# One DMA group moved ahead of another on SyncE, and a higher cap on the products that fill TensorE's idle times

## The chip, the cores and the metric

The kernel runs on one core of a Trainium2 chip. The metric is the device time of one execution in microseconds; lower is better. Five executions of the kernel before gave 496.59, 498.37, 501.29, 503.88 and 504.88, so the median is 501.29.

## The reference

Two blocks follow one another. The first is a delta rule over 4 batches, 8 heads, 768 time steps, with heads 48 wide; the second sends each of the 3072 resulting rows of 384 to one of 8 experts, picked by a hash of its token id.

```python
for t in range(S):
    y[:, :, t] = einsum('bhd,bhde->bhe', q[:, :, t], state)
    v_old = einsum('bhde,bhd->bhe', state, k_n[:, :, t])
    state = state + beta[:, :, t] * einsum('bhd,bhe->bhde', k_n[:, :, t], v[:, :, t] - v_old)
x = y.transpose(0, 2, 1, 3).reshape(3072, 384)
expert = token_ids * 2654435761 % 8
for e in range(8):
    out[expert == e] = maximum(x[expert == e] @ w1[e], 0) @ w2[e]
```

The weights are 8 x 384 x 1024 and 8 x 1024 x 384, all in float32.

## The kernel before, in words

**The delta rule (the first 224 us).** The 768 steps are cut into 24 chunks of 32 steps, and four chunks make a group. The four batches lie side by side on the 128 partitions. Ahead of the chunks of a group come:

- the loads of its keys and queries (`load_turn`, L427 to L431), on SyncE's queue,
- their turning by TensorE against a unit matrix (`turn`, L449 to L463), which ScalarE copies to the tiles KQ,
- the gram products, key by key and query by key (`gram`, L468 to L512; for group 0 `first_gram`, L514 to L539), copied to the tiles GK and GQ, and masked by VectorE,
- the inverse of a triangular matrix per chunk and head, 31 steps of two instructions on VectorE (`inverse`, L572 to L632), and a turning back to the tile TU (L638).

A chunk then is a chain (`chunk`, L672 to L803). TensorE asks the state with the keys (L659) on top of the values (L690), and ScalarE copies the result to R (L695). TensorE multiplies with the inverse (L709), and ScalarE copies W (L723). TensorE updates the state (L738), and ScalarE copies the new state to S (L762). Beside this chain stand the spreading of TU and GQ to Tz and MT (L550), the asking with queries (L659), the answer (L779) and its copy (L788). GpSimd scatters the rows to a scratch tensor in DRAM, ordered by expert (L794). The last four chunks are split in halves, with VectorE's help (L699, L764).

**The planner.** All this isn't issued as written. Each step is noted as a task with an engine, an estimated duration and its dependences (`task`, L253). The function `order` (L286 to L424) plays a list schedule over the estimates, and the tasks are then emitted in the order of their planned starts (L1188 to L1200). The planner also estimates when TensorE's next block of 256 instructions has been loaded. It counts the instructions issued so far in `issued`, and a task whose instructions lie in a block that isn't there yet starts later (L381 to L390).

Where the planner expects TensorE to be idle before a task, `fill` (L320 to L337) puts in products of the unit matrix with itself that nobody reads, 128 to 512 columns wide, as long as an unused PSUM bank is there; they are emitted at L1192.

**The first expert** (`first_expert`, L982 to L1080) runs at the end of this stage, mostly after the last chunk. It takes the first 18 chunks' rows early, and the other rows late. The hidden values of the late part, `h_late`, lie in the same SBUF tile, `xqs[0]` (L144), that later holds the rows of every second expert; the last reader of `h_late` is the product at L1075.

**The other experts (256 to 484 us).** For each expert, `gemm1` (L1222) makes eight blocks of hidden values, each from three products. The max with zero is ScalarE's for even blocks (L1229) and VectorE's for odd ones (L1231). Behind every odd block VectorE also turns a third of the next expert's rows (`turn`, L1290; `turn_x`, L107). Four banks are used in turn, so block 7 needs the bank that VectorE emptied of block 3.

`fetch` (L1283) reads the row at which an expert's rows begin into a register of SyncE, and issues four DMAs for the rows (L100) and one for their numbers (L104). `load_w` (L111) reads which expert it is, and issues four DMAs for w1 (L94) and one for w2 (L117), 384 KB each and 1536 KB. All of these go out on SyncE's queue in program order. Ahead of the loop this order is (L1303 to L1308): rows of the second expert, its weights, weights of the third expert, rows of the third expert, and a register with the number of extra rounds.

The rows of the second expert go to `xqs[1]`; those of the third go to `xqs[0]`.

Of the kernel before, what the change touches and what calls it, by code (L numbers as in the profile page):

```python
# [20 lines left out]
def kernel(  # L21
# [27 lines left out]
    RANKS = [4, 0, 1, 2, 3, 5, 6, 7]  # L49
# [35 lines left out]
    def value(at, engine, top):  # L85
        return nc.values_load(ov_i[0:1, at:at + 1], engines=[engine], min_val=0, max_val=top)

    def expert_at(rank, engine):
        return value(AT_E + rank, engine, E - 1)

    def w1_parts(e, w1_sb, eng):

        w1 = moe_w1[bass.ds(e, 1)].rearrange("o d f -> (o d) f")
        return [lambda j=j: eng.dma_start(  # L94
            out=w1_sb[C * j:C * j + C],
            in_=w1[QD * j:QD * j + QD].rearrange("(c d) f -> d c f", d=C)) for j in range(4)]

    def load_x(row, blocks, xq, eng):
        rows = x_dram[bass.ds(row, C * blocks)].rearrange("(i t) x -> t i x", t=C)
        return [eng.dma_start(out=xq[C * j:C * j + C, 0:blocks, 0:QD],  # L100
                              in_=rows[:, :, QW * j:QW * j + QD]) for j in range(4)]

    def load_numbers(row, cols, width, to, eng):
        return eng.dma_start(out=to, in_=x_dram[bass.ds(row, cols * width), QD:QD + 1].rearrange(  # L104
            "(c p) x -> p c x", c=cols))
# [5 lines left out]
    def load_w(e, pool, eng):  # L111
        s2 = moe_w2[bass.ds(e, 1)].rearrange("o f d -> (o f) d")
        w1_sb = pool.tile([P, CO, F], F32, name="w1_sb")
        for part in w1_parts(e, w1_sb, eng):
            part()
        w2_sb = pool.tile([P, FO, DIN], F32, name="w2_sb")
        eng.dma_start(out=w2_sb, in_=s2.rearrange("(fo p) d -> p fo d", p=P))  # L117
        return w1_sb, w2_sb
# [40 lines left out]
    with ExitStack() as phase1:  # L159
# [126 lines left out]
        def order():  # L286
# [33 lines left out]
            def fill(i, idle, at):  # L320

                nonlocal issued
                rate = 1.67
                if at < 2000:

                    rate, idle = 3.34, idle - 900
                idle = min(idle, 2750 if at < 2000 else 1100)
                while idle > FILL_OVER and at < FILL_UNTIL:
                    unused = [b for b in range(len(homes)) if banks[b] is not None
                              and banks[b] <= at]  # L330
                    if not unused:
                        break
                    n = min(4, max(1, int((idle - 160) / (rate * P))))
                    fills.setdefault(i, []).append((unused[0], n))
                    issued += 2
                    idle -= n * rate * P
                    at += n * rate * P  # L337
# [17 lines left out]
            while len(done) < n:  # L355
                best, can = None, {}
                for e, r in ready.items():
                    can[e] = [(x, i) for x, i in ((when(x, i), i) for x, i in r)
                              if x is not None]
                    if can[e]:  # L360
                        at = max(free[e], min(x for x, _ in can[e]))
                        if best is None or at < best[0]:
                            best = (at, e)
                at, e = best
# [27 lines left out]
                if e == "PE":  # L392
                    fill(pick, s - free[e], free[e])
# [55 lines left out]
        def turn(g, a, b):  # L449
            KQ, src, job = KQs[g % 4], (KTs, QTs)[a][b], new_job(1, early=g < 3)  # L450

            def view():
                return bank(job).rearrange("p (u x) -> p u x", u=HU)

            def go():
                for u in range(HU):
                    nc.tensor.transpose(view()[:, u, :],
                                        src[:, u].rearrange("p r d -> p (r d)"), ident)

            task("PE", 540, (f"t{a}{b}",), (f"j{job}",), go, words=8, job=(job, 0))  # L460
            task("ACT", 490, (f"j{job}",), (f"KQ{g % 4}{a}{b}",),
                 lambda: nc.scalar.activation(KQ[:, :, a, b, :], view(), ACT.Copy),
                 job=(job, 0))  # L463
# [739 lines left out]
    with tc.tile_pool(name="w_pool2", bufs=2) as w_pool2, \  # L1203
# [18 lines left out]
        def gemm1(w1_sb, xT, h_sb, width, between=None):  # L1222
            for fo in range(FO):
                h_ps = hidden()
                for co in range(CO):
                    nc.tensor.matmul(h_ps[:, :width], lhsT=w1_sb[:, co, fo * P:(fo + 1) * P],  # L1226
                                     rhs=xT[:, co, :width], start=(co == 0), stop=(co == CO - 1))
                if fo % 2 == 0:
                    nc.scalar.activation(h_sb[:, fo, :width], h_ps[:, :width], ACT.Relu)  # L1229
                else:  # L1230
                    nc.vector.tensor_scalar(out=h_sb[:, fo, :width], in0=h_ps[:, :width],  # L1231
                                            scalar1=0.0, scalar2=None, op0=ALU.max)
                if between is not None:
                    between(fo)
# [16 lines left out]
        def send_rows(rows, idx, alone):  # L1251
            scat = nc.gpsimd.indirect_dma_start(  # L1252
                out=out[:, :], out_offset=bass.IndirectOffsetOnAxis(ap=idx, axis=0),
                in_=rows, in_offset=None, bounds_check=N - 1, oob_is_err=False)
            if alone:
                tc.declare_no_dep(scat.ins, group="scatters", reason="disjoint rows")
                tc.add_to_no_dep_group("scatters", scat.ins)
# [10 lines left out]
        def send(oT, e, col):  # L1268

            o_ps = results()  # L1270
            cw = CWS[e]
            for i in range(CO):
                nc.tensor.transpose(o_ps[0:cw, i * P:(i + 1) * P],
                                    oT[:, i, col * cw:(col + 1) * cw], ident)
            store(o_ps, col, cw, idx[e][0:cw, col:col + 1], True)
# [4 lines left out]
        def own(e):  # L1280
            return KTS[e], CWS[e], (CAPS[e] + C - 1) // C, xqs[RANKS.index(e) % 2]

        def fetch(e):  # L1283
            cols, cw, blocks, xq = own(e)
            row = value(AT_ROW + e, mybir.EngineType.SP, N)
            load_x(row, blocks, xq, nc.sync)
            xns[e] = m_i.tile([P, KT], F32, name="numbers")
            load_numbers(row, cols, cw, xns[e][0:cw, 0:cols, None], nc.sync)
# [13 lines left out]
        with tc.manual_schedule():  # L1302
            fetch(RANKS[1])  # L1303
            for part in parts:
                part()
            w_tiles[2] = load_w(expert_at(RANKS[2], mybir.EngineType.SP), w_pool2, nc.sync)
            fetch(RANKS[2])
            n_ov = nc.values_load(ov_i[0:1, NOV:NOV + 1], min_val=0, max_val=NOV)  # L1308
            for c in range(CO):
                turn(RANKS[1], c)  # L1310
            for k in range(SC):
                send_rows(o_first[:, k], idx_i[:, k:k + 1], True)
            send_rows(o_late, idx_i[:, SC:SC + 1], True)
            for i, e in enumerate(RANKS):
                if e == FIRST:
                    continue
                w1_sb, w2_sb = w_tiles.pop(i)
                rest = [e for e in RANKS[i + 1:i + 3]]
                done = RANKS[i - 1] if RANKS[i - 1] in oTs else None

                def between(fo):

                    to = max(3, i + 1)
                    if fo == 0 and to < E and to not in w_tiles:
                        w_tiles[to] = load_w(expert_at(RANKS[to], mybir.EngineType.SP),
                                             w_pool if to == 4 else w_pool2, nc.sync)
                    elif fo == 1 and len(rest) > 1:
                        fetch(rest[1])
                    if fo % 2 and fo // 2 < CO and rest:
                        turn(rest[0], fo // 2)  # L1330
                    if fo % 2 and done is not None:
                        send(oTs[done], done, fo // 2)

                h_sb = m_h.tile([P, FO, CAP], F32, name="h_sb")
                gemm1(w1_sb, xTs.pop(e), h_sb, CAPS[e], between)
                if KTS[e] > CO:
                    oTs[e] = m_t.tile([P, CO, CAP], F32, name="oT")
                    for j in range(CO):
                        gemm2_turned(w2_sb, h_sb, oTs[e], j, CAPS[e])
                else:  # L1340
                    cols, cw, _, _ = own(e)
                    for j in range(cols):
                        gemm2(w2_sb, h_sb, j, cw, idx[e][0:cw, j:j + 1], True)
# [49 lines left out]
```

## Time and profile before

| What | us |
|---|---|
| median of five executions | 501.29 |
| the profiled execution, its own time | 498.19 |
| its span, first to last instruction | 496.6 |
| TensorE busy | 460.4 |
| VectorE busy | 230.0 |
| ScalarE busy | 191.6 |
| GpSimd busy | 72.6 |
| mean granted clock of TensorE, as a share of full | 0.969 |

How to read it: busy times are unions of the instructions' spans on an engine. The engines work side by side, so they don't add up to the span. "PE" is TensorE's products and "PEld" its weight loads, "DVE" is VectorE, "ACT" ScalarE, "POOL" GpSimd and "SP" SyncE, whose instructions only issue DMAs. A float32 product stands in the trace as two records (a fill 512 wide is "x2"). An arrow in square brackets names what ended the idle time ahead of an instruction; "issue" means that nothing in the profile did.

### The profile page before, as it was taken

The page shows a single profiled execution, that of the slowest core. Times are in us where ns is not written, and L with a number is a line of the kernel's source. Part 1 is how long each engine was busy: PE and PEld are TensorE (multiplying, and loading weights), DVE is VectorE, ACT ScalarE, POOL GpSimd, SP SyncE. Part 2 cuts the span into 40 slices and gives each one's busy share as a digit, 9 for nine tenths or more (in the row PEclk, how much of TensorE's full clock was granted, in tenths as well). Part 3 has the DMA queues.
Part 4 walks back from the last instruction along what each step waited for, and adds up shares of the span by engine and source line. Part 5 has one row for each costly group of instructions (what it writes and reads, how often), then busy time and mean ns, then how long its engine had stood idle before and what let it go on. Part 6 is the DMA issues. An engine that isn't in the chain of part 4 may idle for free. (4 is left out here: it accounts for less than half of the span.)

```text
span 496.6 us, 15828 instructions
## 1 busy us (share of the span) xinstructions
PE 460.4 (93%) x6648; PEld 312.9 (63%) x6648; DVE 230.0 (46%) x720; ACT 191.6 (39%) x443; POOL 72.6 (15%) x106
## 2 busy tenths in 40 slices
PE   8982898999899999899999999999999999999990
PEld 5761686787677777787765555555555565655650
DVE  5899979998898889860102013012021130110100
ACT  4763778889699687541121011011010110100100
POOL 6000102122020022320020012113011022001010
PEclk9995799999999799999999999999999999999997
DMA  9996767568544457523999995745643016401010
GB/s 143 169 157 114 118 124 143 111 142 159 118 101 93 93 133 174 133 81 81 191 272 244 250 213 154 152 130 111 114 151 74 0 41 164 143 7 39 0 31 15
DMA packets 137181, 60.61 MB, mean 122 GB/s; under 512 B 123006, under 2 KB 131826, under 8 KB 137109
## 3 DMA queue, kind: packets, MB, share of 16 engines
q1 hardware_dynamic: 131572, 49.80, 49.9%
q0 software_dynamic: 5344, 9.66, 6.1%
q8 instruction: 53, 0.87, 0.7%
q10 hardware_dynamic: 192, 0.12, 0.2%
q14 instruction: 20, 0.16, 0.1%
HBM read 49.19 MB, written 10.42 MB: 120 GB/s over the span
## 5 line engine op out<-in xcount | busy, mean ns | idle before, releaser
L1263 PE MATMUL bank<-h_sb,w_sb 128*128 128x424 f32 (+1 forms) x192 | 66.4, 506 | 0.0
L624 DVE TENSOR_TENSOR tmp<-U,Ni 128x87 f32<-128x87 f32 (+15 forms) x186 | 62.5, 341 | 3.5 <-ACT U L608 0.2
L622 DVE TENSOR_TENSOR U<-U,tmp 128x87 f32<-128x87 f32 (+15 forms) x186 | 61.9, 338 | 2.9
L1252 POOL DMA_INDIRECT out_dram<-o_sb,tokens x25 | 29.3, 1171 | 197.8 <-ACT o_sb L1248 152.7
L1226 PE MATMUL z<-xT,w_sb 128*128 128x424 f32 (+3 forms) x168 | 57.4, 491 | 0.0
L1263 PEld LDWEIGHTS bank<-h_sb,w_sb 128*128 128x128 f32 x192 | 36.2, 190 | 28.4 <-issue 15.6
L794 POOL DMA_INDIRECT x_scratch<-x_sb,slot x24 | 24.9, 1039 | 182.7 <-ACT MT L550 58.4
L1231 DVE TENSOR_SCALAR h_sb<-z 128x424 f32<-128x424 f32 (+3 forms) x14 | 7.9, 562 | 88.7 <-PE z L1226 88.7
L1242 PE MATMUL bank<-w_sb,h_sb 128*121 128x384 f32 (+1 forms) x144 | 46.9, 486 | 0.0
L762 ACT ACTIVATE S<-psS 48x384 f32<-48x384 f32 (+1 forms) x92 | 42.7, 464 | 10.1 <-PE psS L738 8.8
L1226 PEld LDWEIGHTS z<-xT,w_sb 128*128 128x128 f32 x168 | 31.6, 190 | 22.2 <-issue 7.5
L1242 PEld LDWEIGHTS bank<-w_sb,h_sb 128*121 128x121 f32 (+1 forms) x144 | 26.6, 185 | 19.4
L779 PEld LDWEIGHTS psY<-W,MT 64*64 64x64 f32 x768 | 25.7, 139 | 10.4 <-issue 8.9
L1265 ACT COPY oT<-bank 128x424 f32<-128x424 f32 (+1 forms) x8 | 4.0, 499 | 71.4 <-PE bank L1263 71.4
L1248 ACT COPY o_sb<-bank 106x384 f32<-106x384 f32 (+3 forms) x14 | 6.7, 478 | 64.0 <-PE bank L1242 49.6
L738 PE MATMUL psS<-W,K 32*128 32x96 f32 x736 | 27.9, 287 | 2.5 <-ACT W L723 2.2
L1226 PE MATMUL psY<-xT,w_sb 128*128 128x424 f32 (+3 forms) x84 | 30.0, 493 | 0.2 <-DVE h_sb L1231 0.2
L1226 PE MATMUL psX<-xT,w_sb 128*128 128x424 f32 (+3 forms) x84 | 29.9, 492 | 0.0
L779 PE MATMUL psY<-W,MT 64*64 64x48 f32 x768 | 29.2, 225 | 0.1
L738 PEld LDWEIGHTS psS<-W,K 32*128 32x128 f32 x736 | 23.8, 192 | 5.7 <-ACT W L723 3.6
L709 PE MATMUL psX<-R,Tz 64*64 64x48 f32 x672 | 24.6, 220 | 0.5 <-issue 0.3
L550 ACT ACTIVATE Tz<-TU,kmask 128x256 f32<-128x256 f32 x40 | 23.8, 718 | 3.3 <-DVE TU L638 3.3
(205 smaller groups left out, 667.7 us busy)
## 6 DMA issues: line engine op xcount, KB each, us to landing
w_sb<-in_moe_w_dram SPq DMA_DIRECT2D x32, 384.0 KB
w_sb<-in_moe_w_dram SPq DMA_DIRECT2D x6, 1536.0 KB
keys<-in_k_dram SPq DMA_DIRECT2D x24, 192.0 KB
Qt<-in_q_dram SPq DMA_DIRECT2D x24, 192.0 KB
V<-in_v_dram SPq DMA_DIRECT2D x96, 48.0 KB
K<-in_k_dram SPq DMA_DIRECT2D x96, 48.0 KB
wide<-in_moe_w_dram SPq DMA_DIRECT2D x8, 384.0 KB
xq<-x_scratch SPq DMA_DIRECT2D x12, 144.0 KB
```

Of the source, the lines that this page charges most:

```text
L550: lambda e=e: nc.scalar.activation(out[:, :, e].rearrange(order_of), in_.rearrange(order_of), ACT.Copy, scale=kmask[:, e:e + 1]))
L622: nc.vector.tensor_tensor(U[:, n:, 0:n], U[:, n:, 0:n], t, op=ALU.add)
L624: nc.vector.tensor_tensor(t, U[:, j:n, 0:n].to_broadcast([P, m, n]), Ni[:, j, n:, None].to_broadcast([P, m, n]), op=ALU.mult)
L709: nc.tensor.matmul(pws[i][rows, h], lhsT=Tz[rows, h].rearrange("p e i -> p (e i)"), rhs=R[rows, h], start=(h == (hs.start if split else 0) ...
L738: nc.tensor.matmul(state[0][:, b, 2 * D * u:2 * D * u + 2 * D], lhsT=K4[quarter(b), u].rearrange("p r d -> p (r d)"), rhs=W[quarter(b), 2 ...
L762: copy = nc.scalar.activation(put, get, ACT.Copy)
L779: nc.tensor.matmul(py[rows, h], lhsT=MT[rows, h].rearrange("p e i -> p (e i)"), rhs=W[rows, h], start=(c == 0 and h == 0), stop=True, skip ...
L794: put = nc.gpsimd.indirect_dma_start(out=x_dram[0:N, :], out_offset=bass.IndirectOffsetOnAxis(ap=slot[:, c:c + 1], axis=0), in_=x_sb, in_o ...
L1226: nc.tensor.matmul(h_ps[:, :width], lhsT=w1_sb[:, co, fo * P:(fo + 1) * P], rhs=xT[:, co, :width], start=(co == 0), stop=(co == CO - 1))
L1242: nc.tensor.matmul(o_ps[0:rows, 0:DIN], lhsT=h_sb[:, fo, col * rows:(col + 1) * rows], rhs=w2_sb[:, fo, :], start=(fo == 0), stop=(fo == F ...
L1252: scat = nc.gpsimd.indirect_dma_start(out=out[:, :], out_offset=bass.IndirectOffsetOnAxis(ap=idx, axis=0), in_=rows, in_offset=None, bound ...
L1263: nc.tensor.matmul(oT_ps[:, 0:width], lhsT=w2_sb[:, fo, i * P:(i + 1) * P], rhs=h_sb[:, fo, 0:width], start=(fo == 0), stop=(fo == FO - 1))
```

## The change

Two places are edited. In `fill` the cap on the idle time that is filled, after the first 2 us, goes from 1100 to 3000 ns of the planner's time. Ahead of the expert loop, the third expert's rows are issued ahead of its weights.

```diff
@@ in order(), fill()
                 if at < 2000:
                     rate, idle = 3.34, idle - 900
-                idle = min(idle, 2750 if at < 2000 else 1100)
+                idle = min(idle, 2750 if at < 2000 else 3000)
                 while idle > FILL_OVER and at < FILL_UNTIL:
...
                     n = min(4, max(1, int((idle - 160) / (rate * P))))
                     fills.setdefault(i, []).append((unused[0], n))
                     issued += 2
                     idle -= n * rate * P
                     at += n * rate * P
@@ ahead of the loop over the experts
             fetch(RANKS[1])
             for part in parts:
                 part()
+            fetch(RANKS[2])
             w_tiles[2] = load_w(expert_at(RANKS[2], mybir.EngineType.SP), w_pool2, nc.sync)
-            fetch(RANKS[2])
             n_ov = nc.values_load(ov_i[0:1, NOV:NOV + 1], min_val=0, max_val=NOV)
```

No input, no result and no tile size changes. In the built program the first edit gives TensorE 10 filling products instead of 7. The three more count in `issued`, and from chunk 3 to chunk 15 (and once in the last four chunks) the planner's order of the tasks is another one on every engine but GpSimd. The second edit moves five DMAs and the register loads ahead of them on SyncE's queue.

## The prediction

> **What bounds the kernel now.** I read the page first, then busy time by stretch, then the timeline at each place that the change touches. The profiled execution took 498.19 us (span 496.6 and 1.6 around it); the five runs have a median of 501.29, which is 3.1 higher. The sum below is made against 498.19, and 3.1 is added at the end.
>
> ```profile
> PE   8982898999899999899999999999999999999990
> ...
> PEclk9995799999999799999999999999999999999997
> ...
> q8 instruction: 53, 0.87, 0.7%
> ```
>
> TensorE is busy nearly everywhere but in slice 4 (37 to 50 us), and its clock is down in slices 4, 5 and 14. From 255.98 to 484 TensorE runs the experts with one gap of 0.18 us, so there only TensorE's own work counts. Ahead of that lie two stages. In the first, up to the first chunk, it is VectorE that never rests (columns: stretch, length, PE, PEld, DVE, ACT, POOL busy, clock, DMA share, GB/s):
>
> ```profile
> 25.00:30.00 5.00, 3.90 (x187) 2.56 (x187) 5.00 (x24) 2.55 (x12) 0.00 (x0) 1.00 1.04 166
> 30.00:35.00 5.00, 4.43 (x132) 3.91 (x133) 5.00 (x22) 4.03 (x14) 0.00 (x0) 1.00 0.96 161
> ...
> 40.00:45.00 5.00, 2.20 (x136) 1.96 (x136) 5.00 (x21) 1.26 (x6) 0.00 (x0) 0.50 0.49 86
> ```
>
> That work is the inverse of group 0 (L613 to L638), a serial chain from the first gram products to the first W:
>
> ```profile
> 9.57 0.60 ACT L462 ACTIVATE KQ<-bank 128x512 f32<-128x512 f32 x1 [0.87 <-PE bank L457]
> ...
> 10.75 1.12 PE L1192 MATMUL z<-ident 128*128 128x512 f32 x2
> ...
> 12.62 0.19 PE L525 MATMUL psX<-KQ 48*32 48x32 f32 x1 [0.53 <-issue]
> ...
> 13.79 1.09 DVE L537 COPY GK<-psY 128x512 f32<-128x512 f32 x1 [2.13 <-PE psY L525]
> ...
> 47.98 1.24 DVE L638 STREAM_TRANSPOSE TU<-U 128x1024 f32<-128x1024 f32 x1
> ...
> 52.55 0.49 ACT L723 ACTIVATE W<-psX 128x384 f32<-128x384 f32 x1 [0.19 <-PE psX L709]
> ```
>
> See that the last gram products could have begun at 10.8 (KQ is ready at 10.2). A filling product runs first, then five records at 11.81 to 11.89, and a stop until 12.62 that nothing in the profile releases ("issue"). The queue named instruction moved 0.87 MB in 53 transfers, 16.4 KB each; I take the stop for one of those. VectorE idles 2.13 us for these products, and then hardly again until 47.98.
>
> The second stage, 52.5 to 224, is 24 chunks: W, state update, S, R, next W, with gram and turning products between, TensorE 90% to 100% busy.
>
> **The change part by part.**
>
> *1. Fills.* The order of built instructions shows three products more: after the 512-wide one at 10.75, another of 512 and one of 256; after the 512-wide one at 25.88, one of 256. From the rows, 10.75 to the next start at 11.81, a 512-wide one takes 1.06 us, so 256 takes 0.53. The first place: the fills end at 11.81 + 1.06 + 0.53 = 13.40. The stop until 12.62 lies under them. The products that ran at 11.81 to 11.89 and 12.62 to 13.55, 1.01 us in all, run from 13.40 to 14.41 instead of ending at 13.55: +0.86. VectorE's copy at 13.79 moves as much, and with VectorE full from 20 to 50 us nothing absorbs it before W at 52.55; the chunks follow as a chain, so +0.86 reaches the end. Bounds: 0, if the chunks' own gaps (8.0 us of gaps over 0.12 us from 60 to 224) swallow it; +1.59, if nothing stops at 12.62.
>
> The second place, +0.53: the next users are the copies of GK at 28.39 to 32 us, which VectorE takes at 39.38. Cover 7 us; cost 0. The nearest other user is the masking at 30.84, whose copies end by 30.04 at the latest: 0.8 us of cover. If both went, 0.5.
>
> The Trainium skill ("Runtime: NRT & Kernel Launch", section "Instruction fetch mechanics") says that instructions come in 16 KiB blocks of 256 and that crossing into the next is mostly hidden. The size agrees with the 16.4 KB; the hiding doesn't agree with the 0.53 us. By the page the fills would be pure delay, +1.59, and the forecast 502.8 instead of 502.1; I go by the row.
>
> *2. The planner's order.* Each fill also counts in the planner's account of issued instructions (`issued += 2`, L335), so its guesses of block starts move, and it picks another order on all engines from chunk 3 to chunk 15 (chunks count from 0). The amount of work is equal: 768 gram products and 192 turning products, all built ahead of the update of chunk 14, in both. In before, the chunks 7, 8, 9, 10 hold 0, 24, 40, 64 gram products, in after 32, 32, 64, 0; chunks 13 and 14 hold 32 and 96 against 40 and 88. So this work is spread a chunk earlier and as densely. I take 0, since both the work and its peaks are alike. The bounds come from what such an order can win or lose in this trace. From 100 to 176 TensorE's gaps add up to 3.6 us, and there is one stretch of half clock:
>
> ```profile
> 160.00:165.00 5.00, 4.01 (x202) 3.26 (x182) 4.72 (x17) 2.66 (x8) 0.00 (x0) 1.00 0.65 152
> 165.00:170.00 5.00, 4.97 (x105) 3.49 (x105) 4.12 (x11) 3.20 (x8) 0.00 (x0) 0.53 0.44 104
> ```
> ```profile
> 165.44 0.49 ACT L723 ACTIVATE W<-psX 128x384 f32<-128x384 f32 x1 [1.06 <-PE psX L709]
> ...
> 174.69 0.49 ACT L723 ACTIVATE W<-psX 128x384 f32<-128x384 f32 x1 [0.69 <-PE psX L709]
> ...
> 182.27 0.49 ACT L723 ACTIVATE W<-psX 128x384 f32<-128x384 f32 x1 [0.44 <-PE psX L709]
> ```
>
> The chunk under half clock takes 9.3 us and the next, with as little gram work, 7.6; those after it 6.4. A stretch costs 1.7 to 2.9 us. The clock fell after gaps of no more than 0.73 and 0.30 us (ahead of 162.78 and 165.03), so a new order can lose it, or keep it, without any long gap. Both ways: 3.6 + 2.9 = 6.5 won at most, the same lost if gaps and stretch come twice.
>
> The Trainium skill ("TensorE: Matmul & The Clock Gate", section "HAM oscillation — how this bites in real kernels") lets the clock fall after more than about 3.4 us idle, and prices the time at half clock at one half of it. The trace disagrees, with a fall after 0.73 and 0.30 us. By the page a new order with gaps of this size could neither lose nor win a stretch, the bounds of this part would shrink to 3.6 either way, and the sum would stay.
>
> *3. The end of the chunks.* In one of the last chunks (update at 213.25) after puts half of the answer (8 of the 16 of L779; 1.07 us for all, so 0.53) between the halves of the update, and one product of the first expert (L1041) behind them. The copies of S wait for both halves: +0.53. The moved product, 0.43 us from start to start at 226 us, then runs in a wait and is gone from the full stretch after 224: -0.43. Together +0.10 (bounds -0.43 and +0.53).
>
> *4. The third expert's rows.* Before: weights issued 243.12 to 249.3, then SyncE waits for the last reader of the tile that also holds the late part's hidden values (L1075), then the rows:
>
> ```profile
> 248.91 0.39 SPq L117 DMA_DIRECT2D w_sb<-in_moe_w_dram  x1
> ...
> 256.18 7.03 SPq L100 DMA_DIRECT2D xq<-x_scratch  x4
> ...
> 270.08 0.65 DVE L108 STREAM_TRANSPOSE xT<-xq 128x448 f32<-128x448 f32 x1 [8.96 <-DMA xq<-x_scratch]
> ```
>
> The rows land at 270.0, behind 3.1 MB of weights; VectorE's turning waits 8.96, its next max stands behind it, and TensorE waits 0.18 (the gap ahead of 271.27). After: the rows are first in line at 256.2. The queue is empty by then, since the second expert's 3.1 MB, issued by 242.1, takes 12.3 us at the 250 GB/s of these rows. The second expert's rows, in a like place, issued at 233.14 and turned at 238.88, took 5.7; so these land near 262, when the turning first wants them (261.1): -0.18.
>
> What pays: five DMAs of weights, with their register loads, stand behind the wait. They start at 259 (rows in 1.89 and 0.28, as at 233.14) to 265.5 (7.03 as now), take 5 to 7 us to issue and 12.3 to move, and land by 274 to 283. The third expert's first product is due 17 us after 273.2, at 290.2. Cover 7 us or more: cost 0. The fourth expert's weights and rows and the count's load, next in the queue, move by 2 to 7 us. In before the fourth's rows are issued by 279.4 and first turned at 295.57, and TensorE needs that turning's bank only about 10 us later; cost 0. POOL's scatters are not moved past anything.
>
> *Sum.* 498.19 + 0.86 + 0 + 0.10 - 0.18 = 498.97, or +0.78; with 3.1 for the median, **502.1 us**.
>
> **The rivals.**
>
> *A, slower: the new order loses the clock.* Chunks 9 and 14 with 64 and 88 narrow products bring further stretches at half clock, as at 165. For it: the fall at 165 came in just such a packed place. Against: 127 to 135 is as packed and had none. One costs 1.7 to 2.9; over 1% takes 506.3 - 502.1 = 4.2, so it decides from the second on. Two at 2.5: 507.1.
>
> *B, faster: the new order closes the gaps.* Gram work a chunk earlier, so that chunk 14 no longer drops the clock (-2.9) and most of 3.6 us of gaps goes: 502.1 - 6.5 = 495.6. For it: chunk 14 holds 88 instead of 96. Against: chunk 9 now holds 64.
>
> *C, slower: weights late.* If the third expert's weights landed at 295 or later, TensorE would wait 5 us at 290: 507. Against: 7 us of cover at the worse bound.
>
> *D: the first fill's delay is swallowed.* Then +0.78 becomes -0.08: 501.2, no change either.
>
> **How the numbers follow.** A change of 1% (5.0 us) is about what a measurement of this kernel can tell from none, as its five runs lie between 496.6 and 504.9. Forecast and D, within 1%: 0.50 (0.35 and 0.15), own range 497 to 506. A: 0.28, C: 0.03, together slower 0.31. B: 0.19. A outweighs B because part 1 already leans 0.8 us that way and the packed places are no fewer. The range goes by the bounds of part 2 around the sum, 6.5 each way, and so holds B's end and A's two stretches: 495.5 to 508.5. Beyond it lie A with three stretches and C with a later landing, 1 in 10, and on the other side B together with D, 1 in 10.
>
> **What would show it.** Part 1: the first gram products end at 14.4, W at 53.4. Part 2: W of chunk 17 (188.64 in before) 0.9 us later; if it is over 3 us off either way, look for PEclk under 1.00 between 86 and 176. Part 4: the turning ahead of 262 no longer waits 9 us, TensorE has no gap at 271, and 290 shows no wait for weights. I am wrong if W of chunk 17 moves by more than 4 us, or if TensorE waits after 256.

## The result

The changed kernel takes 496.29 us (median of 48 runs, 494.25 to 500.46); beside it the kernel before takes 499.78 (90 runs). The ratio is 0.9949 with a 95% interval of 0.9934 to 0.9963. So the change wins 0.5%, some 2.5 us, where the forecast's sum had +0.78. The time lies inside the range that the forecast gave (495.5 to 508.5), but the change lies on the other side of zero, and the interval is narrow enough to say so.

A ratio leaves out the runs that lie over 1.5% above the fastest of their kernel, and it isn't the quotient of the two medians, which is 0.9930 here.

The profiled execution took 501.09 us (span 499.5), longer than any of the 48 timed runs, so its total says nothing; its places do. From its page, TensorE's busy share and its clock in 40 slices:

```profile
PE   8982899999999998999999999999999999999990
...
PEclk9996799999999798899999999999999999999996
```

Slice 14 is down to 7 as before, so the new order didn't keep the clock at 165 us. Slices 16 and 17 are down as well: a second stretch, 196.0 to 202.8, which before didn't have. Such a stretch differs from one execution to the next: in e5's, the same kernel again, neither of the two is there, and the span is 494.1.

The first chain: the copy of GK, and W of the chunks 0, 15, 16 and 17 (chunk 15's W answers to the 174.69 shown of before).

```profile
9.73 0.60 ACT L462 ACTIVATE KQ<-bank 128x512 f32<-128x512 f32 x1 [0.87 <-PE bank L457]
...
10.92 2.42 PE L1192 MATMUL z<-ident 128*128 128x512 f32 x6
13.26 0.21 PE L525 MATMUL psX<-KQ 48*32 48x32 f32 x1
...
14.54 1.09 DVE L537 COPY GK<-psY 128x512 f32<-128x512 f32 x1 [2.88 <-PE psY L525]
...
52.99 0.49 ACT L723 ACTIVATE W<-psX 128x384 f32<-128x384 f32 x1 [0.20 <-PE psX L709]
...
173.80 0.49 ACT L723 ACTIVATE W<-psX 128x384 f32<-128x384 f32 x1 [0.81 <-PE psX L709]
181.38 0.49 ACT L723 ACTIVATE W<-psX 128x384 f32<-128x384 f32 x1 [0.44 <-PE psX L709]
187.75 0.49 ACT L723 ACTIVATE W<-psX 128x384 f32<-128x384 f32 x1 [0.86 <-PE psX L709]
```

The fills stand in one row of 2.42 us, the stop of 0.53 us is gone under them, and the copy of GK comes 0.75 us later. W of chunk 0 comes 0.44 us later (52.55 before), W of chunk 17 0.89 us earlier (188.64 before); in e1, which has the same order, it comes 0.64 us later, so one profile doesn't tell.

The third expert's rows. SyncE's queue and VectorE's turnings:

```profile
259.62 2.13 SPq L100 DMA_DIRECT2D xq<-x_scratch  x4
261.94 0.28 SPq L104 DMA_DIRECT2D numbers<-x_scratch  x1
263.72 3.17 SPq L94 DMA_DIRECT2D w_sb<-in_moe_w_dram  x4
267.08 0.39 SPq L117 DMA_DIRECT2D w_sb<-in_moe_w_dram  x1
```
```profile
265.96 0.65 DVE L108 STREAM_TRANSPOSE xT<-xq 128x448 f32<-128x448 f32 x1 [1.40 <-DMA xq<-x_scratch]
268.68 0.64 DVE L108 STREAM_TRANSPOSE xT<-xq 128x448 f32<-128x448 f32 x1
```

The turning waits 1.40 us instead of 8.96, and TensorE has no gap after the second expert's first product. The weights are all issued by 267.5, and the third expert's first product (293.58) follows on the work before it without a wait.

### The profile page after: what moved, and what is told of

Its sections match the earlier page's. It is cut to its first block, busy times and chain, and to the rows that moved or that the text cites. A ratio compares the mean times of both kernels' runs of the same rounds, so it can differ in the third digit from the quotient of the medians.

```text
span 499.5 us, 15849 instructions
## 1 busy us (share of the span) xinstructions
PE 463.6 (93%) x6654; PEld 315.8 (63%) x6654; DVE 229.2 (46%) x720; ACT 192.5 (39%) x443; POOL 71.7 (14%) x106
## 5 line engine op out<-in xcount | busy, mean ns | idle before, releaser
L1226 PE MATMUL z<-xT,w_sb 128*128 128x424 f32 (+3 forms) x168 | 57.4, 491 | 0.0
L1226 PEld LDWEIGHTS z<-xT,w_sb 128*128 128x128 f32 x168 | 31.6, 190 | 22.2 <-issue 7.6
L1226 PE MATMUL psX<-xT,w_sb 128*128 128x424 f32 (+3 forms) x84 | 29.9, 492 | 0.0
L1226 PE MATMUL psY<-xT,w_sb 128*128 128x424 f32 (+3 forms) x84 | 29.9, 491 | 0.0
L1231 DVE TENSOR_SCALAR h_sb<-psY 128x424 f32<-128x424 f32 (+3 forms) x14 | 7.9, 565 | 40.7 <-PE psY L1226 40.7
```

## The experiments

Every ratio is against the kernel before on the same chip, with its 95% interval. e1 to e4 ran on one chip, e5 to e8 on a second, e9 to e12 on a third (where every kernel is some 6 us longer) and e13 to e16 on a fourth. The kernel before has 7 filling products, the change 10. "Old" is the planner's order of before, "new" that of the change.

| run | added products | order | rows | ratio | interval |
|---|---|---|---|---|---|
| the change | yes | new | ahead | 0.9949 | 0.9934 to 0.9963 |
| e1 | yes | new | behind | 0.9992 | 0.9951 to 1.0033 |
| e2 | no | old | ahead | 0.9977 | 0.9938 to 1.0016 |
| e3 | yes | old | behind | 1.0043 | 1.0004 to 1.0083 |
| e4 | no | new | behind | 0.9998 | 0.9958 to 1.0038 |
| e5 | yes | new | ahead | 0.9919 | 0.9879 to 0.9959 |
| e6 | yes | new | behind | 0.9960 | 0.9927 to 0.9994 |
| e7 | no | new | ahead | 0.9914 | 0.9884 to 0.9943 |
| e8 | no | old | later still | 1.0032 | 0.9995 to 1.0070 |
| e9 | yes | old | ahead | 0.9973 | 0.9948 to 0.9998 |
| e10 | yes | new | ahead | 0.9940 | 0.9909 to 0.9970 |
| e11 | no | old | ahead | 0.9972 | 0.9942 to 1.0001 |
| e12 | no | new | ahead | 0.9926 | 0.9897 to 0.9955 |
| e13 | no | old, last four chunks new | ahead | 0.9995 | 0.9963 to 1.0027 |
| e14 | no | new | ahead | 0.9959 | 0.9921 to 0.9997 |
| e15 | others, 9 in all | a third | ahead | 0.9937 | 0.9897 to 0.9976 |
| e16 | others, 8 in all | a fourth | ahead | 0.9974 | 0.9941 to 1.0006 |

**One part at a time (e1 to e4).** Three theories stood against each other: the new order gains (T1), the moved rows gain (T2), the added products keep the clock up early (T3). e1 is the change without its second edit, e2 the second edit alone.

> Only the bound on idle time is raised (1100 to 3000); the third expert's rows stay behind its weights. Theory T1 (the planner's new order is the gain): 0.995 of before, and W of the chunk numbered 17 starts at least 0.8 us earlier against W of chunk 0 than in before. T2 (the moved rows are the gain): 1.000 to 1.002, and the turning at 270 us waits about 9 us as in before. T3 (the added products hold the clock up in the first stage): 0.995, with W of chunk 0 no later than 52.6 us.

> Only the third expert's rows go ahead of its weights; filling products and planner's order are those of before. T1: 0.9996 to 1.000 (the 0.18 us of one gap at 271 us, no more). T2: 0.995, so the rows' lateness costs far more than 0.18 us in typical executions than in the profiled one. T3: 0.9996 to 1.000.

e3 issues the added products but leaves them out of the planner's account; e4 counts them and doesn't issue them:

```diff
@@ e3
-                idle = min(idle, 2750 if at < 2000 else 1100)
+                counted = min(idle, 2750 if at < 2000 else 1100)
+                idle = min(idle, 2750 if at < 2000 else 3000)
...
-                    issued += 2
+                    if counted > FILL_OVER:
+                        issued += 2
+                    counted -= n * rate * P
@@ e4
-                idle = min(idle, 2750 if at < 2000 else 1100)
+                real = min(idle, 2750 if at < 2000 else 1100)
+                idle = min(idle, 2750 if at < 2000 else 3000)
...
-                    fills.setdefault(i, []).append((unused[0], n))
+                    if real > FILL_OVER:
+                        fills.setdefault(i, []).append((unused[0], n))
                     issued += 2
+                    real -= n * rate * P
```

> The three added products are issued but not counted in the planner's account, so the order of all other work is that of before; the rows stay. T1: 1.0015 (+0.75 us, the delay of the copy of GK, carried to the end). T2: 1.0015 too. T3: 0.995, with the first stretch of half clock shorter than the 17.07 us of before.

> The three added products are counted in the planner's account, so the order is that of the changed kernel from chunk 3 on, but they are not issued; the rows stay. T1: 0.993 to 0.995 (the gain of the order without the 0.75 us that the first added product costs). T2: 1.000. T3: 1.000, with the first stretch of half clock as long as in before.

None of the four alone reaches 0.9949, so T1 as expected (0.993 to 0.995 for e4) and T3 (0.995 for e3) fall; e2 lies between what T1 and T2 expected, and its interval holds both. T1's mark isn't met either: from W of chunk 0 to W of chunk 17 e1 takes 0.38 us less than before, and e4 1.14 more. e3 is slower than before, by 0.4%, clear of zero but only just.

The profiles say more than the ratios. TensorE at the place of the gap at 271 us, one line each from before, e1, e3 and e4 (start, duration, the wait ahead in brackets):

```profile
271.27 2.40 PE L1226 MATMUL psY<-xT,w_sb 128*128 128x424 f32 x6 [0.18 <-DVE h_sb L1231]
```
```profile
274.77 2.40 PE L1226 MATMUL psY<-xT,w_sb 128*128 128x424 f32 x6 [2.17 <-DVE h_sb L1231]
```
```profile
275.94 2.40 PE L1226 MATMUL psY<-xT,w_sb 128*128 128x424 f32 x6 [0.47 <-DVE h_sb L1231]
```
```profile
276.25 4.06 PE L1226 MATMUL psY<-xT,w_sb 128*128 128x424 f32 x6 [2.55 <-DVE h_sb L1231]
```

The gap that the profiled execution of before showed as 0.18 us is 0.47 in e3 and 2.17 and 2.55 in e1 and e4, the two with the new order. So the lateness of the rows is a race whose margin differs from one execution to the next, and in these profiles it is worse with the new order.

**The rows put back, and pushed further (e5 to e8).** e5 is the change itself, e6 is e1 once more, e7 is e4 with the rows ahead. e8 is the kernel before with 0.39 MB more in front of the rows:

```diff
@@ e8
             w_tiles[2] = load_w(expert_at(RANKS[2], mybir.EngineType.SP), w_pool2, nc.sync)
+            spare = m_q.tile([P, 2, DIN], F32, name="spare")
+            nc.sync.dma_start(out=spare, in_=moe_w2[0].rearrange("(fo p) d -> p fo d", p=P)[:, 0:2])
             fetch(RANKS[2])
```

> The changed kernel itself, measured beside the next three. Theory M (moved rows are the gain): 0.995, no gap of TensorE between 270 and 277 us. Theory O (planner's order is the gain): 0.995 too.

> The changed kernel with the one line of the rows put back behind the third expert's weights (as in e1, a second measurement). M: TensorE waits about 2.2 us for the rows again (2.18 in e1, 2.55 in e4), so the ratio is 0.004 to 0.005 above that of the changed kernel beside it. O: the same as the changed kernel, 0.995.

> The changed kernel without its three added products: planner's order and moved rows as in the changed kernel. M and O both: 0.0015 below the changed kernel beside it (0.75 us of the copy of GK), so about 0.9935, if the added products are pure delay; equal to it, if they are hidden after all.

> The kernel before, with 0.39 MB of weights loaded once more, into a tile nobody reads, between the third expert's weights and its rows; at 250 GB/s this puts the rows 1.6 us later. M: every microsecond of it is one of TensorE's, so the gap ahead of the turned rows is 1.7 to 4.2 us where it was 0.18 to 2.55, and the ratio is 1.003. O: 1.000, since the rows would not be on the path in a typical execution.

M (the rows) came out in its ratios: putting one line back takes the change from 0.9919 to 0.9960, and pushing the rows back costs 0.3% (the interval of e8 reaches 0.9995). The gap of e6 is smaller than expected, 1.25 us for 2.2; that of e8 is 1.99, as expected. e7 is equal to the change, so the 0.0015 of the added products doesn't show. VectorE's first turning and TensorE's line of the gap, of e6 and then of e8:

```profile
272.31 0.65 DVE L108 STREAM_TRANSPOSE xT<-xq 128x448 f32<-128x448 f32 x1 [10.03 <-DMA xq<-x_scratch]
```
```profile
273.49 2.40 PE L1226 MATMUL psY<-xT,w_sb 128*128 128x424 f32 x6 [1.25 <-DVE h_sb L1231]
```
```profile
272.02 0.65 DVE L108 STREAM_TRANSPOSE xT<-xq 128x448 f32<-128x448 f32 x1 [10.77 <-DMA xq<-x_scratch]
```
```profile
273.21 3.41 PE L1226 MATMUL psY<-xT,w_sb 128*128 128x424 f32 x6 [1.99 <-DVE h_sb L1231]
```

Set beside each other, the profiles with the rows behind give one rule for the gap. "Due" counts from the second expert's first product to the turning, "landing" from the issue of the second expert's rows (L100, 233.14 in before) to the turning, "reach" from that issue to the first product. "Expert stage" is the time from that first product to the end of the last L1226.

| | before | e3 | e8 | e6 | e1 | e4 |
|---|---|---|---|---|---|---|
| order | old | old | old | new | new | new |
| reach | 22.84 | 23.55 | 23.35 | 22.21 | 22.34 | 22.21 |
| landing | 36.95 | 37.94 | 39.27 | 37.38 | 38.45 | 38.69 |
| due | 14.10 | 14.39 | 15.92 | 15.18 | 16.10 | 16.48 |
| gap of TensorE | 0.18 | 0.47 | 1.99 | 1.25 | 2.17 | 2.55 |
| expert stage | 212.89 | 213.17 | 216.40 | 213.96 | 214.89 | 216.92 |

The gap is due less 13.92 in all six, within 0.02. Landing varies by 1.7 us between executions (36.95 to 38.69; e8's 39.27 less the 1.57 of its 0.39 MB is 37.70). Reach depends on the order: 23.2 on the mean of the six profiles of the old one that e1 to e12 and before give (22.77 to 23.55), 22.2 on the mean of eight of the new one (22.04 to 22.36). So TensorE comes 1.0 us earlier, counted from the issue of the rows. Of this, 0.43 is the one product less behind W of chunk 23 (part 3); the other 0.55 is no gain of TensorE, since the rows go out later there (10.41 us after W of chunk 23 on the mean, for 9.86).

The expert stage is 212.44 us in all twelve profiles with the rows ahead. Behind them it is longer by the gap, by 0.27, and in e4 and e8 by another 1.7: there TensorE's clock fell at the end of the gap. The same stretch of 5 us in e4 and in e1 (columns as in the prediction's first table of stretches; TensorE's clock is the third number from the end):

```profile
275.00:280.00 5.00, 3.75 (x6) 2.04 (x7) 2.93 (x7) 0.00 (x0) 0.00 (x0) 0.66 1.03 216
```
```profile
275.00:280.00 5.00, 5.00 (x15) 2.68 (x15) 2.12 (x6) 0.00 (x0) 0.00 (x0) 1.00 1.03 204
```

**The order, with the rows ahead (e9 to e12).** e9 is e3 with the rows ahead, so the change with the old order; e10 is the change, e11 is e2, e12 is e7.

> The changed kernel with the planner's order of before: the three added products issued but not counted, the rows ahead. Theory N (the new order itself gains, since it loses less time at half clock in the chunks): 0.004 to 0.005 above the changed kernel beside it, mean granted clock 0.004 lower. Theory R (the order gains nothing, the rows are all): equal to the changed kernel, within 0.002, at the same clock.

> The changed kernel, as the measure for its three neighbours. N and R: 0.992 to 0.995, mean granted clock 0.972, no gap of TensorE after 256 us.

> Rows moved, order of before, no added products. N: 0.996 to 0.998 and 0.003 to 0.005 above e12. R: equal to e12.

> Rows moved, the new order, no added products. N: 0.991 to 0.994. R: equal to e11. Of the added products: equal to the changed kernel within 0.0015, the first stretch of half clock 17.07 us long and not 13.65, W of chunk 0 at the same distance (38.5 us) from the copy of GK.

With the rows ahead the new order is 0.0033 below the old one with the added products and 0.0046 without them. Each of these differences is about as large as the intervals. N's numbers come out; its reason is open. The mean clock of e9 and e10 is 0.9716 and 0.9723, not 0.004 apart, and that of e11 and e12 0.9700 and 0.9725. The added products move nothing that these ratios resolve (e9 against e11 +0.0001, e10 against e12 +0.0014).

**All of e1 to e12 together.** One pair of kernels is too noisy for half a per cent, but the design is crossed, so all runs can be used at once. A least-squares fit to the 200 runs behind the ratios of before and e1 to e12 (without e8), with one term for each of the three chips and one for each part of the change, gives:

| part | us | 95% interval |
|---|---|---|
| rows ahead | -2.4 | -3.0 to -1.8 |
| new order | -1.3 | -1.9 to -0.7 |
| added products | +0.4 | -0.2 to +1.0 |

A term for the new order and the moved rows together comes out at -0.3, with 1.2 either way, so the two are not shown to be worth more together than apart. The three parts add up to -3.3, against the 2.5 that the change itself showed, which is within their intervals. The same fit of the mean clock puts the new order 0.0025 higher, with 0.0014 either way: less time at half clock may be part of its gain.

**Other counts, other orders (e13 to e16).** The planner's count starts elsewhere, with the rows ahead and the old cap; 66 gives exactly the new order. Counts of 68 and 74 also change the fills: TensorE has 9 and 8 filling products there, not 7.

```diff
-            issued, begun, have = 60, [], 900.0
+            issued, begun, have = 66, [], 900.0
```

> Rows ahead, no added products, but the planner's count of issued instructions starts at 62 instead of 60: another order between, the last four chunks as in before. If the chunk stage's gain of the new order is its own, this lies with the old order, 0.997; if the gain is the last chunks' (the product moved behind them), 0.997 too, with 33.19 us from W of chunk 23 to the second expert's first product as in before; if any new order draws anew from a spread, anything from 0.990 to 1.000.

> The count starts at 66: this gives exactly the new order of the changed kernel (that of e7 and e12), rows ahead, no added products. 0.990 to 0.994 if the new order gains with the rows ahead; 0.997 if the order gains nothing.

> The count starts at 68: a third order, different on POOL and SyncE's queue as well; rows ahead. Spread of orders: anything from 0.990 to 1.000; if the order does not matter, 0.997.

> The count starts at 74: a fourth order; rows ahead. Spread of orders: anything from 0.990 to 1.000; if the order does not matter, 0.997.

e13's kernel is not what its expectation says, but the reverse. Its trace has the old order up to the last four chunks, and the new one in these: 10.7 us from W of chunk 21 to W of chunk 23, and 32.76 from there to the second expert's first product, as in the change. So e13 and e14 differ only in the order of the chunks 3 to 15. The means of their twelve runs are 501.19 and 498.84 us, 2.4 apart with a 95% interval of 0.7 to 4.0. So this pair puts the gain of the new order into the chunks 3 to 15, and not into the last four.

Counts of 62, 66, 68 and 74 give 0.9995, 0.9959, 0.9937 and 0.9974, 0.6% apart, with the old order (0.9972 to 0.9977) in the middle. But the new order alone, in three kernels without the added products on three chips, gives 0.9914, 0.9926 and 0.9959, so a spread of this size between single ratios is little more than noise. That orders differ like draws from a spread is a reading that fits, and isn't shown.

## Why the prediction was wrong

**The step that failed is part 4, "-0.18".** The mechanism was right: rows in line behind 3.1 MB, the turning 9 us late, TensorE waiting for the bank that VectorE had not emptied. The size was one execution's margin. The wait of 8.96 us had already used up its cover to the last 0.18 us, so any later landing was TensorE's at full price. What the runs showed in its place is -2.4 us, with 0.6 either way (the fit above). With the old order moving the rows wins 0.23% and 0.28% (e2, e11: 1.3 us), with the new one 0.41% (e5 against e6) and 0.43% (the change against e1): 2.1 us. The expert stage of the five profiles with the rows behind is longer than 212.44 by 0.45 (before), 0.73 (e3), 1.52 (e6), 2.45 (e1) and 4.48 (e4), 1.9 on the mean. So the profile that the forecast was made from had the smallest of five, and the term left out the spread of the landing, the 0.27, and the clock that can fall at the gap.

**Part 2, "I take 0", failed too.** The new order measured -1.3 us, with 0.6 either way. With the rows ahead it gains 0.3% to 0.5% (e9 and e10, e11 and e12). With the rows behind the ratios don't agree: without the added products it shows nothing (e4 0.9998), with them it is 0.5% below the old order on the same chip (e1 against e3), and e6 is at 0.9960. The profiles with the rows behind suggest that a gain ahead of the experts is lost again in the race for the rows, since the gap is 1.25 to 2.55 with the new order and 0.18 and 0.47 with the old one; the runs neither show this nor exclude it. The bounds of 6.5 held the term. The equal amount of work and the equal peaks were no reason for 0; they were a reason for not knowing. Where in the chunks 3 to 15 the gain lies isn't settled: from W of chunk 3 to W of chunk 17 the old order takes 111.7 us (mean of six profiles, 109.3 to 114.0) and the new one 110.6 (nine, 107.3 to 113.5), which the spread doesn't tell apart.

**Part 1, +0.86, was right up to the first chunk.** From the first copy of KQ to the copy of GK the seven profiles with the added products take 9.36 us on the mean (8.96 to 10.00), and the seven without them, up to e12, 8.57 (8.05 to 9.33): +0.79. The stop at 12.62 is not fixed either: 0.93 us in e4, 0.61 in e7, none in e2, nor in any profile with the added products. To W of chunk 0 +0.64 is left. The second fill's 0 was right: from the copy of GK to W it is 38.46 to 38.50 us in all profiles with the added products. Whether the delay reaches the end isn't shown: the fit has +0.4, with 0.6 either way.

**Part 3, +0.10, measured +0.33.** W of chunk 21 to W of chunk 23 takes 9.9 us in before and 10.7 in the change (+0.77, forecast +0.53). From there to the first product of the second expert it takes 33.19 and 32.76 (-0.43, as forecast). e13 has this part alone, beside the moved rows, and shows no gain.

**The covers.** The weights' lateness cost nothing, as said: no wait at 290, and 212.44 us in every profile with the rows ahead.

**The rivals.** A didn't happen: no kernel with the new order and the rows ahead lies above before. B's time (495.6) is near what was measured by luck: it stood 5.7 us below a median of five runs, 501.29, which is 1.5 above that of the 90. Its reason isn't seen in the profile after: the stretch of half clock at 165 us is still there, and TensorE's gaps of over 0.12 us between W of chunk 3 and of chunk 17 add up to 5.42 us against 4.77. C didn't happen. D had the delay swallowed and only the rows' -0.18 left; the profiles still show +0.64 of the delay at W of chunk 0.

T3's mechanism exists without a gain that shows. Half clock ahead of W of chunk 1 lasts 13.65 us in five of seven profiles with the added products and 17.07 in all seven without them up to e12, but VectorE, which is busy without a break there, sets the end.

**The best version.** The changed kernel without its added products (e7, e12, e14) is at 0.9914, 0.9926 and 0.9959, with the change itself at 0.9919 beside e7 and 0.9940 beside e12. It isn't shown to be faster than the change; both beat the kernel before.

## What to carry to other kernels

When a wait on a transfer has just eaten its whole cover, its visible price in one profile (here 0.18 us) is a sample of a race, and not the price: take the spread of the transfer's landing over several profiles, and what makes the other runner arrive earlier. Here five profiles had 0.45 to 4.48 us, and moving the rows was worth 2.4. An edit that feeds a list schedule with one more count changes the order of everything behind it, and that was worth 1.3 us here: give it a term with a range and no sign, and not a zero. And where single ratios differ by less than their intervals, cross the parts of a change and use all runs at once before telling one part from another.

## What was not expected of the hardware

The length of a gap alone didn't decide whether the clock fell: 1.99 us in e8 was followed by half clock, 2.17 us in e1 wasn't. All stretches of half clock are multiples of 3.41 us, but for the last of each trace, which its end cuts; so their ends give a grid of windows 3.41 us long. In e4 (gap 273.70 to 276.25) and e8 (271.21 to 273.21) the gap lay inside one window (e4's but for its last 0.04 us), 272.80 to 276.21 and 271.05 to 274.46 on the grid of each execution, and the next window was at half clock. In e1 the gap (272.60 to 274.77) was cut by the grid at 273.09, and in e6 it lay inside one window (271.85 to 275.26) but was 1.25 us long; neither cost clock. So these four gaps fit a rule by the idle time within one window. No run tests it, and the fall at 165 us, after gaps of 0.72 and 0.30 us, isn't explained by it.

The Trainium skill ("TensorE: Matmul & The Clock Gate", section "HAM oscillation — how this bites in real kernels") wants more than about 3.4 us of idle time for a fall. Here 2.55 and 1.99 us were enough. Its price, half of the throttled time, agrees with the trace: half of 3.41 is 1.71, and e4's expert stage is 4.48 us longer, of which the gap and the 0.27 leave 1.66 (1.70 in e8).
